# A spectral-mixing stage whose matmuls read each input column four times and write 64 columns instead of 16

## The chip, the cores and the metric

The kernel runs on one core of a Trainium2 chip. The core has a matrix engine (TensorE, in the profile PE for the matmuls and PEld for the loads of their stationary operand), a vector engine (VectorE, DVE), a scalar engine (ScalarE, ACT), GpSimd (POOL), a queue engine (SyncE, SP) and 16 DMA engines. The metric is the device time of one execution in microseconds (us), the median of several executions. The kernel before took 380.24 us (three executions, 378.93 to 380.4).

## The reference

Two stages run one after the other on `x`, 8 batches of 5696 positions and 128 features. The first is a long convolution with `h`, done by FFT. The second is a spectral mixing: the first 64 modes of the real FFT along the sequence are each multiplied by their own complex 128 x 128 matrix, the result goes back through the inverse FFT, is added to its input, and a gated linear layer is added to that.

```
Xf = rfft(x, n=2*S); Hf = rfft(h, n=2*S)
x  = irfft(Xf * Hf)[:, :S]                       # S = 5696
X  = rfft(x);  Xr, Xi = X[:, :64].real, X[:, :64].imag
Yr = einsum('bmd,mde->bme', Xr, w_r) - einsum('bmd,mde->bme', Xi, w_i)
Yi = einsum('bmd,mde->bme', Xr, w_i) + einsum('bmd,mde->bme', Xi, w_r)
u  = x + irfft(Y, n=S)                           # Y is zero above mode 64
out = u + relu(u @ w_ch)
```

## The kernel before

The FFTs are products with constant matrices. The sequence is split into 89 rows of 64 positions, and the two steps of the transform, the pointwise product with the filter and the way back are all matmuls with fp16 operands and fp32 sums in PSUM. PSUM has eight banks of 512 fp32 values in each of 128 partitions; every result is copied out of it by ACT or DVE (the helper `evac`, lines 301 to 314).

The program is written as one list of operations for each engine in the order of the code. A `Recorder` (lines 21 to 121) notes what each operation reads and writes by name (a PSUM bank is `("bank", i)`) and puts in the semaphore waits that follow. So the order of the matmuls on PE is the order of the calls, and a matmul that needs a bank waits until the engine that was to read the bank has done so. All matmuls go through the helper `mm`, so nearly all have line 320 in the profile, and are told apart by their operands' names.

The stages are, in order: the transform of `h` (`ps<-F,Hp`), four groups of two batches, each with the transform of `x` and the convolution (`ps<-F,Xin`, `ps<-As,M`, `ps<-U,Wc`) and the gathering of the 64 modes (`ps<-G,Zs`), and the last part, from about 257 us on. There the modes of all batches lie in the tile XT: for each batch 192 values in a row, the imaginary parts with changed sign, the real and the imaginary ones, 64 each.

The change is made at the start of that last part, in lines 770 to 798. `reflect` fills the second half of two constant tiles (S4a on DVE, S4b on ACT). `mix(m0, m1)` does the mixing: for each mode two matmuls with the mode's 128 x 128 matrices from the tile W as stationary operand (`ps<-XT,W`). The moving operand is read out of XT with the step from batch to batch: 8 batches, 192 fp16 values (384 bytes) apart, for the real and the imaginary part, 16 columns in all. The 16 columns that come out lie next to one another in bank 6 (modes 0 to 31) or bank 7 (32 to 63). In between PE does parts of the way back from the convolution, `u_z` (`ps<-S4a,ZT0a` and `ps<-S4b,ZT0b`, 89 columns each), for three tiles ahead, in banks 0 to 5. Two copies, one on ACT and one on DVE, bring the mixed modes of a bank to the tile Y (`Y<-ps`). Then eight transposes (line 791, `ps<-Id,Y`) turn Y into banks 6 and 7, two more copies scale this into the tile C, and from there `u_tile` and `o_tile` alternate until the end: the way back of the modes is added (`ps<-IBs,C`, 356 columns), the sum is copied to UT, and the gated layer (`ps<-WI,UT`) and the output follow. The first column blocks of `u_z` go to the slots of two banks 0, 2, 4, 6 in turn (`LSLOT`), so the third tile ahead has banks 4 and 5.

GpSimd and SP issue DMAs only here: GpSimd loads the gated layer's weights and the tiles ZT3 and ZT4, SP later loads and the output.

Of the kernel before, what the change touches and what calls it, by code (L numbers as in the profile page):

```python
# [4 lines left out]
P = 128  # L5
# [8 lines left out]
RELU = mybir.ActivationFunctionType.Relu  # L14
# [109 lines left out]
def bass_long_conv_fft__then__afno_spectral_mix_kernel(nc, x, h, moe_w_r, moe_w_i, moe_w_ch, out):  # L124
    B, S, D = x.shape
    M = moe_w_r.shape[0]
# [79 lines left out]
    def at(name, cols, dt, off):  # L206
        return nc.alloc_sbuf_tensor_at(name, [P, cols], dt, offset=off)
# [41 lines left out]
    XTW = 3 * M  # L249
    xt = at("XT", B * XTW, F16, a_g + GW * 2 + 2048 * (NZX - NZ))  # L250
# [24 lines left out]
    NR = len(r_off)  # L275
    r_sb = [at(f"R{i}", 512, F32, r_off[i]) for i in range(NR)]
    w_sb = at("W", 2 * M * D, F16, a_x)
    y_sb = at("Y", 2 * B * M, F16, r_off[0])
# [10 lines left out]
    def pv(bank, off, dims, p0=0, n=P):  # L289
        return bass.AP(ps, p0 * 4096 + bank * 512 + off, [[4096, n]] + [list(d) for d in dims])  # L290

    R = Recorder(nc)
# [3 lines left out]
    def bank(i):  # L296
        return ("bank", i)
# [3 lines left out]
    def evac(dst, src, reads, writes, scale=None, eng=None, after=()):  # L301
        e = eng
        if e is None:
            turn[0] ^= 1
            e = "scalar" if turn[0] else "vector"
        if e == "scalar":
            if scale is None:
                R.add(e, lambda h_: h_.copy(dst, src), reads, writes, after=after)  # L308
            else:
                R.add(e, lambda h_: h_.activation(dst, src, COPY, scale=scale), reads, writes, after=after)  # L310
        elif scale is None:
            R.add(e, lambda h_: h_.tensor_copy(dst, src), reads, writes, after=after)  # L312
        else:
            R.add(e, lambda h_: h_.tensor_scalar_mul(dst, src, scale), reads, writes, after=after)  # L314

    def dma(eng, dst, src, ring, reads=(), writes=(), after=()):
        R.add(eng, lambda h_: h_.dma_start(dst, src), reads, writes, ring=ring, after=after)  # L317

    def mm(o, l, r, st, sp, reads, writes):
        R.add("tensor", lambda h_: h_.matmul(o, l, r, start=st, stop=sp), reads, writes)  # L320
# [3 lines left out]
    def once(key, toks):  # L324
        if key in first:
            return []
        first[key] = 1
        return list(toks)
# [3 lines left out]
    def turns(name, items):  # L332
        i = ring2.get(name, 0)
        ring2[name] = i + 1
        return items[i % len(items)]
# [80 lines left out]
    for j in range(16):  # L416
        t = turns("h", [0, 2, 4])
        for i in range(8):
            d = 8 * j + i
            for r in range(2):  # L420
# [6 lines left out]
             eng="vector" if j % 4 == 1 else "scalar")  # L427
# [69 lines left out]
    G_ALL = [("g", i) for i in range(NG)]  # L497
    WT = [("w", i) for i in range(NWP)]
    ZY = [("zs", i, b) for i in range(NZL, NZX) for b in range(2)]
# [18 lines left out]
    def reflect(eng, t, n, col, key, after):  # L518
        MN = S - SH
        dst, src = bass.AP(t, SH, [[S, n], [1, MN]]), bass.AP(t, SH - NQ - 1, [[S, n], [-1, MN]])  # L520
        sc = sg_sb[0:n, col:col + 1]
        if eng == "scalar":
            R.add(eng, lambda e: e.activation(dst, src, COPY, scale=sc), [key + (0,), ("sg",)], [key + (1,)], after=after)
        else:
            R.add(eng, lambda e: e.tensor_scalar_mul(dst, src, sc), [key + (0,), ("sg",)], [key + (1,)], after=after)
# [201 lines left out]
    def u_z(i, b, half, alone=False, parts=(0, 1)):  # L727
        g_, c_ = divmod(i, NCH)
        t = ahead.get((i, b, half))
        if t is None:  # L730
            t = turns("l", LSLOT)
        z = zt[i % NC]
        for hb in parts:
            if not alone:
                u_c(i, b, half, t, hb, True)
            for pl in range(4):
                for ri in range(2):
                    pz = half * 8 + hb * 4 + pl
                    so = (c_ * ZB + pz) * NQ
                    n = (P, PB + RB)[ri]  # L740
                    mm(pv(t + hb, pl * NQ, [[1, NQ]]), z[ri][0:n, pz * 256 + b * P:pz * 256 + b * P + P], s4_sb[ri][0:n, so:so + NQ],
                       alone and pl == 0 and ri == 0, not alone and pl == 3 and ri == 1, [("zt", i % NC, ri), ("zt0", i % NC), ("s4", ri, 0)] + ([("s4", ri, 1)] if c_ >= NCH // 2 else []), [bank(t + hb)])
        if alone:
            ahead[(i, b, half)] = t
        return t
# [24 lines left out]
    XTT = [(n, g_) for g_ in range(NP) for n in ("xt", "xtn")]  # L770
    reflect("vector", s4_sb[0], P, 0, ("s4", 0), M_ALL[1:4])
    reflect("scalar", s4_sb[1], PB + RB, 1, ("s4", 1), AST)
    def mix(m0, m1):
        for m in range(m0, m1):
            for ri, first_col in ((0, M + m), (1, m)):
                mm(pv(6 + m // 32, m % 32 * 2 * B, [[1, 2 * B]]), w_sb[:, (ri * M + m) * D:(ri * M + m + 1) * D],
                   bass.AP(xt, first_col, [[B * XTW, P], [M, 2], [XTW, B]]), ri == 0, ri == 1, WT + XTT, [bank(6 + m // 32)])

    u_z(0, 0, 0, True)
    for n in range(2):  # L780
        mix(16 * n, 16 * n + 16)
        u_z(0, 0, 1, True, (n,))
    mix(32, M)
    u_z(0, 1, 0, True, (0,))
    for hb in range(2):
        evac(bass.AP(y_sb, hb * 32 * B, [[2 * M * B, P], [B, 32], [M * B, 2], [1, B]]),
             pv(6 + hb, 0, [[2 * B, 32], [B, 2], [1, B]]), [bank(6 + hb)], [("y", hb)], eng="vector" if hb else "scalar",
             after=ZY)
    for b in range(B):
        bk = 6 + b // 4  # L790
        R.add("tensor", lambda e, b=b, bk=bk: e.transpose(  # L791
            ps16[:, bk * 1024 + (b % 4) * P:bk * 1024 + (b % 4) * P + P], bass.AP(y_sb, b, [[2 * M * B, P], [B, P]]), id_sb[:, :]),
              [("y", 0), ("y", 1), ("id",)], [bank(bk)])
    u_z(0, 1, 0, True, (1,))
    for hb in range(2):
        evac(c_sb[:, hb * 512:hb * 512 + 512], ps16[:, (6 + hb) * 1024:(6 + hb) * 1024 + 512], [bank(6 + hb)],
# [11 lines left out]
    def o_tile(g_, b, r4):  # L808
        ub = (g_ % 2) * 2 + b
        bb = 2 * g_ + b  # L810
        t = turns("l", LSLOT)
        i = n_o[0]
        n_o[0] += 1
        full = r4 < NW // 4
        last_ = (g_, b) == (NP - 1, 1)
        wide = r4 < (8 if last_ else NW // 4 // 2 * 2)
        big = wide or (last_ and full)
        h_ = r4 % 2 if wide else 0
        if big:
            if not h_:  # L820
                o_cur[0] = turns("o8", list(range(NO8)))
            ob, key, old = o8_sb[o_cur[0]], ("o8", o_cur[0]), o8_old[o_cur[0]]
        else:
            k_ = turns("os", list(range(NO)))
            ob, key, old = o_sb[k_], ("os", k_), o_old[k_]
        OW = 1024 if big else 512
        n, rows = (4, P) if full else (1, TAIL)
        rd = [("u_", ub, c_) for c_ in range(2 * NCH)] + [("wch",), ("i16",)]
        for j in range(n):
            lh = bass.AP(u_sb[ub], 4 * r4 + j, [[S, P], [NW, P]]) if full else u_sb[ub][:, NW * P:S]  # L830
            mm(pv(t + j // 2, (j % 2) * 256, [[1, 256]], 0, rows), lh, WI, True, True, rd, [bank(t + j // 2)])
        bk = [bank(t), bank(t + 1)] if full else [bank(t)]
        rs = r_sb[i % NR]
        rv = bass.AP(rs, 0, [[512, rows], [P, n], [1, P]])
        ov = bass.AP(ob, h_ * 512, [[OW, rows], [P, n], [1, P]])
        src_r, src_u = pv(t, 0, [[256, n], [1, P]], 0, rows), pv(t, P, [[256, n], [1, P]], 0, rows)
        R.add("scalar", lambda e: e.activation(rv, src_r, RELU), bk, [("r", i % NR)], after=once(("r", i % NR), G_ALL + XTT + [("y", 0), ("y", 1), ("id",)]))  # L837
        R.add("vector", lambda e: e.tensor_tensor(ov, src_u, rv, ADD), bk + [("r", i % NR)],  # L838
              [key + (h_,)], after=once(key, old))
        if wide and not h_:  # L840
            return
        w_ = (2 if wide else 1) * 4 * D
        if full:
            dst = bass.AP(out.tensor, out.offset + bb * S * D + (4 * r4 - 4 * h_) * D, [[NW * D, P], [1, w_]])
            src = ob[:, 0:w_]
        else:
            dst = bass.AP(out.tensor, out.offset + bb * S * D + NW * P * D, [[D, TAIL], [1, D]])
            src = ob[0:TAIL, 0:P]
        dma("sync", dst, src, "o", [key + (v_,) for v_ in range(h_ + 1)])
# [4 lines left out]
    for g_ in range(NP):  # L854
        last = g_ == NP - 1
        order = [(c_, b) for b in range(2) for c_ in range(NCH)] if last else [(c_, b) for c_ in range(NCH) for b in range(2)]
        for n, (c_, b) in enumerate(order):
            i = NCH * g_ + c_
# [10 lines left out]
    while todo:  # L869
        o_tile(*todo.pop(0))  # L870
# [32 lines left out]
```

## Time and profile before

| | |
|---|---|
| median of three executions | 380.24 us |
| profiled execution, its own time | 383.51 us |
| profiled execution, span | 381.7 us |
| busy: PE, PEld | 363.6 us (95%), 280.4 us (73%) |
| busy: DVE, ACT, POOL | 303.7 us (80%), 311.9 us (82%), 83.9 us (22%) |
| mixing matmuls (`ps<-XT,W`) | 128, first start 257.7 us, last start 262.1 us |
| copies to Y | ACT 585 ns, DVE 693 ns |
| chain that ended last | PE 82%, ACT 9%, DVE 6% |

The profile is of one execution. "Busy" counts the time in which an engine has an instruction in flight. Matmuls overlap, so the time from the start of one to the start of the next is shorter than the duration of one, and a PE that is always busy need not be at its peak. PEclk is the TensorE clock that was granted, as a share of the full one. A group's row shows the line, the engine, the operation, the tile written and the tiles read, the shapes, the number of instructions, the busy time in us and the mean duration of one in ns, and behind the second bar the idle time of the engine before them and what ended it.

### The profile page before, as it was taken

The numbers are of one execution on the slowest core, as the hardware profiler recorded it, in microseconds if no ns is written. First come the engines' busy times: TensorE is split into PE (matmuls) and PEld (weight loads), VectorE is DVE, ScalarE is ACT, GpSimd is POOL, SyncE is SP. The second block draws the span as 40 slices with busy tenths as digits, with TensorE's granted clock in tenths as the row PEclk, the third lists the DMA queues.
The fourth block names the chain that finished last, engine by engine and source line by source line (L and its number), as shares of the span: only waits on it lengthen the run. The fifth ranks groups of instructions, "written<-read, shape, count | busy, mean of one in ns | idle before, by whom it ended". The sixth has DMA issues, their size and how long they took to land.

```text
span 381.7 us, 11950 instructions
## 1 busy us (share of the span) xinstructions
PE 363.6 (95%) x5107; PEld 280.4 (73%) x5107; DVE 303.7 (80%) x331; ACT 311.9 (82%) x492; POOL 83.9 (22%) x137
## 2 busy tenths in 40 slices
PE   7998989999989999999999899999999999999992
PEld 4898856667856667766668666668898988888871
DVE  7566998998988998889998888766347766777784
ACT  8357989998989998999998899994466777777783
POOL 8400012320823311822203211339000000000000
PEclk9997999999999999999999999996899999999997
DMA  7998589998999996999996599999999999999867
GB/s 137 201 280 349 140 228 227 276 269 238 107 134 228 234 269 167 143 129 250 235 283 119 137 298 251 300 328 406 407 388 402 402 415 414 404 408 378 342 256 313
DMA packets 84560, 103.92 MB, mean 272 GB/s; under 512 B 22126, under 2 KB 68974, under 8 KB 81538
## 3 DMA queue, kind: packets, MB, share of 16 engines
q1 hardware_dynamic: 59643, 67.73, 51.3%
q0 software_dynamic: 24864, 35.43, 44.3%
q8 instruction: 40, 0.66, 0.7%
q14 instruction: 13, 0.11, 0.1%
HBM read 70.61 MB, written 51.12 MB: 319 GB/s over the span
## 4 chain that ended last, share of the span: by engine, by line
PE 82%; ACT 9%; DVE 6%; issue 1%; DMA 0%; DVEq 0%
PE ps L320 82%; ACT As L310 7%; DVE As L314 2%; DVE U L597 1%; DVE Hs L312 1%; ACT R L837 0%; DMA F<-cF 0%; DVE UT L312 0%; ACT UT L308 0%; ACT XT L310 0%; DVE O L838 0%; PE ps L791 0%; ACT Hs L308 0%; DVE Os L838 0%; ACT Ah L310 0%
## 5 line engine op out<-in xcount | busy, mean ns | idle before, releaser
L320 PE MATMUL ps<-U,Wc 128*128 128x512 f16 (+1 forms) x368 | 95.8, 384 | 0.0
L605 DVE TENSOR_TENSOR U<-Xs,Hs 128x2048 f16<-128x2048 f16 (+1 forms) x68 | 80.7, 1189 | 11.5 <-ACT Xs L308 10.0
L308 ACT CAST Xs<-ps 128x1024 f16<-128x1024 f32 (+1 forms) x72 | 69.5, 971 | 7.8 <-PE ps L320 4.8
L838 DVE TENSOR_TENSOR O<-ps,R 128x512 f32<-128x512 f32 x81 | 52.5, 686 | 19.8 <-ACT R L837 12.5
L308 ACT CAST Zs<-ps 128x512 f16<-128x512 f32 (+1 forms) x126 | 66.0, 604 | 0.0
L837 ACT ACTIVATE R<-ps 128x512 f32<-128x512 f32 x96 | 50.9, 573 | 14.6 <-PE ps L320 14.1
L314 DVE TENSOR_SCALAR As<-ps 128x720 f16<-128x720 f32 (+1 forms) x60 | 50.1, 879 | 9.1 <-PE ps L320 8.0
L310 ACT ACTIVATE As<-ps 128x720 f16<-128x720 f32 (+1 forms) x72 | 51.6, 772 | 6.6 <-PE ps L320 5.7
L320 PE MATMUL ps<-F,Xin 128*128 128x180 f16 x512 | 54.5, 255 | 2.6 <-ACT Ah L310 1.0
L320 PEld LDWEIGHTS ps<-F,Xin 128*128 128x128 f16 x512 | 46.8, 156 | 9.3 <-DVE As L314 2.6
L320 PE MATMUL ps<-WI,UT 128*128 128x256 f16 x360 | 52.5, 281 | 0.5 <-DVE O L838 0.4
L320 PE MATMUL ps<-As,M 64*128 64x128 f16 x1440 | 48.9, 217 | 4.3 <-DVE U L597 3.5
L320 PEld LDWEIGHTS ps<-U,Wc 128*128 128x128 f16 x368 | 28.5, 98 | 28.5 <-ACT Zs L308 6.1
L320 PEld LDWEIGHTS ps<-As,M 64*128 64x128 f16 x1440 | 40.5, 94 | 10.9 <-DVE U L597 4.2
L317 POOL DMA_DIRECT2D Xt<-in_x_dram x48 | 24.8, 520 | 102.9 <-PE ps L320 102.2
L605 DVE TENSOR_TENSOR U<-ps,Hs 128x2048 f16<-128x2048 f32 x20 | 45.7, 2283 | 0.0
L308 ACT CAST UT<-ps 128x712 f16<-128x712 f32 x40 | 30.0, 752 | 18.7 <-PE ps L320 18.7
L320 PEld LDWEIGHTS ps<-WI,UT 128*128 128x128 f16 x360 | 39.5, 152 | 4.4 <-issue 2.2
L320 PE MATMUL ps<-IBs,C 128*128 128x356 f16 x128 | 40.8, 328 | 0.4
L320 PEld LDWEIGHTS ps<-G,Zs 128*128 128x128 f16 x492 | 27.3, 97 | 13.3
L308 ACT CAST Zt<-ps 128x512 f16<-128x512 f32 (+1 forms) x58 | 31.0, 606 | 0.1
L320 PE MATMUL ps<-G,Zs 128*128 128x2 f16 (+2 forms) x492 | 30.5, 192 | 0.0
(88 smaller groups left out, 500.3 us busy)
## 6 DMA issues: line engine op xcount, KB each, us to landing
out_dram<-O SPq DMA_DIRECT2D x39, 512.0 KB, 10.4
zscr<-Zs SPq DMA_DIRECT2D x60, 256.0 KB, 6.3
Xt<-in_x_dram POOLq DMA_DIRECT2D x24, 320.0 KB, 6.9
zscr<-Zt SPq DMA_DIRECT2D x28, 256.0 KB, 6.6
W<-wscr POOLq DMA_DIRECT2D x8, 512.0 KB, 5.3
M<-cM POOLq DMA_DIRECT2D x5, 720.0 KB, 20.3
ZT0a<-zscr SPq DMA_DIRECT2D x3, 1024.0 KB, 13.4
Xr<-in_x_dram POOLq DMA_DIRECT2D x8, 320.0 KB, 13.8
```

What stands on the lines that cost most here:

```text
L308: R.add(e, lambda h_: h_.copy(dst, src), reads, writes, after=after)
L310: R.add(e, lambda h_: h_.activation(dst, src, COPY, scale=scale), reads, writes, after=after)
L312: R.add(e, lambda h_: h_.tensor_copy(dst, src), reads, writes, after=after)
L314: R.add(e, lambda h_: h_.tensor_scalar_mul(dst, src, scale), reads, writes, after=after)
L317: R.add(eng, lambda h_: h_.dma_start(dst, src), reads, writes, ring=ring, after=after)
L320: R.add("tensor", lambda h_: h_.matmul(o, l, r, start=st, stop=sp), reads, writes)
L597: R.add("vector", lambda e, b=b, s_=s_: e.tensor_tensor(bass.AP(u_s[i], b * 512, [[2048, P], [1024, 2], [1, n * D]]), s_, hv, MULT), [tok, ...
L605: R.add("vector", lambda e: e.tensor_tensor(uv, src, hv, MULT), bk + [("h", t, 0), ("h", t, 1, 0), ("h", t, 1, J)], [("u", i)])
L837: R.add("scalar", lambda e: e.activation(rv, src_r, RELU), bk, [("r", i % NR)], after=once(("r", i % NR), G_ALL + XTT + [("y", 0), ("y", 1 ...
L838: R.add("vector", lambda e: e.tensor_tensor(ov, src_u, rv, ADD), bk + [("r", i % NR)], [key + (h_,)], after=once(key, old))
```

## The change

The mixing's moving operand gets a further dimension of four with a step of zero, so each matmul reads its 16 columns four times and writes 64. The copies lie 64 columns apart in the bank, at the place of the modes four, eight and twelve later, which are written after it in the same bank; the last ones reach beyond the sixteenth mode. 16 modes go to a bank instead of 32, so the mixing uses banks 4 to 7. Four copies to Y of 256 columns each, alternating between ACT and DVE and each behind its 16 modes, take the place of two copies of 512 columns behind all modes. The transposes wait for all four, and the first use of a tile that lies over Y is ordered behind all four.

```
+    MQ = M // 4
+
     def mix(m0, m1):
         for m in range(m0, m1):
             for ri, first_col in ((0, M + m), (1, m)):
-                mm(pv(6 + m // 32, m % 32 * 2 * B, [[1, 2 * B]]), w_sb[:, (ri * M + m) * D:(ri * M + m + 1) * D],
-                   bass.AP(xt, first_col, [[B * XTW, P], [M, 2], [XTW, B]]), ri == 0, ri == 1, WT + XTT, [bank(6 + m // 32)])
+                mm(pv(4 + m // MQ, m % MQ * 2 * B, [[8 * B, 4], [1, 2 * B]]), w_sb[:, (ri * M + m) * D:(ri * M + m + 1) * D],
+                   bass.AP(xt, first_col, [[B * XTW, P], [0, 4], [M, 2], [XTW, B]]), ri == 0, ri == 1, WT + XTT, [bank(4 + m // MQ)])
+
+    def y_out(q):
+        evac(bass.AP(y_sb, q * MQ * B, [[2 * M * B, P], [B, MQ], [M * B, 2], [1, B]]),
+             pv(4 + q, 0, [[2 * B, MQ], [B, 2], [1, B]]), [bank(4 + q)], [("y", q)], eng="vector" if q % 2 else "scalar",
+             after=ZY)
 
     u_z(0, 0, 0, True)
     for n in range(2):
-        mix(16 * n, 16 * n + 16)
+        mix(MQ * n, MQ * n + MQ)
+        y_out(n)
         u_z(0, 0, 1, True, (n,))
-    mix(32, M)
+    for n in range(2, 4):
+        mix(MQ * n, MQ * n + MQ)
+        y_out(n)
     u_z(0, 1, 0, True, (0,))
-    for hb in range(2):
-        evac(bass.AP(y_sb, hb * 32 * B, [[2 * M * B, P], [B, 32], [M * B, 2], [1, B]]),
-             pv(6 + hb, 0, [[2 * B, 32], [B, 2], [1, B]]), [bank(6 + hb)], [("y", hb)], eng="vector" if hb else "scalar",
-             after=ZY)
     for b in range(B):
         bk = 6 + b // 4
         R.add("tensor", lambda e, b=b, bk=bk: e.transpose(
             ps16[:, bk * 1024 + (b % 4) * P:bk * 1024 + (b % 4) * P + P], bass.AP(y_sb, b, [[2 * M * B, P], [B, P]]), id_sb[:, :]),
-              [("y", 0), ("y", 1), ("id",)], [bank(bk)])
+              [("y", q) for q in range(4)] + [("id",)], [bank(bk)])
```

More of the change, by code (lines that the diff above doesn't have):

```diff
@@ L836, in o_tile @@
         src_r, src_u = pv(t, 0, [[256, n], [1, P]], 0, rows), pv(t, P, [[256, n], [1, P]], 0, rows)
-        R.add("scalar", lambda e: e.activation(rv, src_r, RELU), bk, [("r", i % NR)], after=once(("r", i % NR), G_ALL + XTT + [("y", 0), ("y", 1), ("id",)]))
+        R.add("scalar", lambda e: e.activation(rv, src_r, RELU), bk, [("r", i % NR)], after=once(("r", i % NR), G_ALL + XTT + [("y", q) for q in range(4)] + [("id",)]))
         R.add("vector", lambda e: e.tensor_tensor(ov, src_u, rv, ADD), bk + [("r", i % NR)],
```

## The prediction

> **What bounds the kernel now.** I read the page first, then the chain of waits in order of time, then the busy time by stretches around the mixing, and last the groups with their shapes kept apart. The page:
>
> ```profile
> span 381.7 us, 11950 instructions
> PEclk9997999999999999999999999996899999999997
> ```
>
> The chain that ended last, in order of time (start, length, what):
>
> ```profile
> 257.70 5.23 PE ps L320 x152
> 262.93 0.23 issue
> 263.16 1.05 PE ps L791 x8
> 264.21 29.32 PE ps L320 x437
> ```
>
> PE itself is the bound from the mixing on: four further pieces of 9 to 13 us follow with gaps below 0.1 us, up to 343 us, and most of what is left is PE too. No wait of PE in this stretch is for a DMA. So what PE gains or loses between 257.7 and 268.4 us reaches the end nearly whole. In the clock's row the slices from 257.6 to 276.7 us stand out (6 and 8). The stretches, for PE alone the first three numbers (length, busy, count), then PEld, DVE, ACT, POOL, the granted clock, DMA share and GB/s:
>
> ```profile
> 22.68:26.10 3.42, 3.42 (x63) 3.42 (x61) 2.19 (x3) 1.94 (x3) 0.00 (x0) 0.95 1.05 259
> 26.10:29.51 3.41, 2.46 (x43) 2.37 (x42) 1.50 (x2) 1.91 (x3) 0.00 (x0) 0.95 0.99 405
> 29.51:32.92 3.41, 3.41 (x24) 3.41 (x25) 1.73 (x2) 1.78 (x3) 0.00 (x0) 0.50 1.03 428
> ...
> 258.20:261.62 3.42, 3.42 (x114) 3.42 (x111) 2.92 (x1) 2.21 (x2) 3.42 (x4) 0.95 1.06 427
> 261.62:265.03 3.41, 3.18 (x51) 2.86 (x48) 1.48 (x3) 0.60 (x1) 3.41 (x5) 0.50 1.00 400
> 265.03:268.44 3.41, 3.41 (x25) 2.27 (x24) 1.33 (x3) 1.41 (x2) 2.94 (x3) 0.50 1.07 389
> 268.44:271.86 3.42, 3.42 (x64) 3.06 (x63) 1.78 (x2) 1.15 (x2) 0.00 (x0) 0.95 1.06 423
> ```
>
> The clock falls to 0.50 at 261.6 us and comes back at 268.4, a stay of 6.8 us; the only other stay before the end is 29.5 to 32.9, half as long, and the two beginnings are 68 times 3.41 us apart. PE is *busy* throughout 258.20 to 261.62, and the clock falls all the same: 98 of its 114 matmuls have 16 columns, and 98 x 16 + 16 x 89 = 2992 columns at 0.42 ns (slope below) fill 1.25 us, 37% of the stretch. Before the other fall it was 43 x 90 x 0.42 = 1.6 us, 48%, where 70% (63 matmuls) had kept the clock in the stretch before. So what counts is not whether PE is busy but how much of the time columns pass.
>
> **What a column costs.** Durations of groups, shapes kept apart (count, busy us, mean ns):
>
> ```profile
> L320 PE MATMUL ps<-IBs,C 128*128 128x356 f16 x21 | 6.6, 315 | 0.0
> L320 PE MATMUL ps<-G,Zs 128*128 128x128 f16 x246 | 28.7, 216 | 0.0
> L320 PE MATMUL ps<-G,Zs 128*128 128x2 f16 x152 | 15.5, 166 | 0.0
> L320 PE MATMUL ps<-XT,W 128*128 128x16 f16 x128 | 4.3, 192 | 0.1
> ...
> L320 PEld LDWEIGHTS ps<-WI,UT 128*64 128x64 f16 x8 | 0.8, 106 | 1.2 <-issue 1.0 <-ACT UT L308 0.2
> L320 PEld LDWEIGHTS ps<-F,Hp 128*64 128x64 f16 x256 | 15.2, 214 | 0.3 <-issue 0.3
> ```
>
> The first (from 270 to 280 us, at full clock) to third read adjacent columns: (315 - 166) / 354 = 0.42 ns a column on a base of 165. Sixteen such columns would take 172 ns; the mixing's take 192. They lie 384 bytes apart in XT. So each costs 0.42 + 20/16 = 1.69 ns, four times an adjacent one. Loads of the stationary operand show the same: 64 adjacent columns 106 ns, 64 columns 260 bytes apart (Hp) 214, 1.69 ns more for each; for 128 columns it is 98 (Wc) against 156 (Xin), 0.45 ns more each.
>
> ```profile
> 260.24 1.98 PEld L320 LDWEIGHTS ps<-XT,W 128*128 128x128 f16 x64
> 260.28 2.05 PE L320 MATMUL ps<-XT,W 128*128 128x16 f16 x64
> 262.37 0.69 DVE L312 CAST Y<-ps 128x512 f16<-128x512 f32 x1 [1.25 <-PE ps L320]
> 263.13 0.82 PEld L791 LDWEIGHTS ps<-Id,Y 128*128 128x128 f16 x8 [0.41 <-issue]
> ```
>
> From the timeline: the 64 starts are (2.05 - 0.19) / 63 = 29.5 ns apart, which is 27 ns for the columns and 2.5 between matmuls. After the fall the last of them, from 261.87 us on, start every 26 to 27 ns, not every 55: the slow reading does not go by PE's clock. Nor does the load of Xin: 156 ns in the whole trace, 167 at 0.50, where adjacent loads go from 98 to 151.
>
> **The change part by part.** *64 columns in place of 16.* The repeat reads the same 384-byte steps again, so I count 64 x 1.69 = 108 ns and 2 between, 110 ns a matmul while the clock is full and 107 when it is half (27 ns for 16 columns there). Bounds from the rows: with 0.45 ns extra a column, 64 x 0.87 + 2.5 = 58 ns; with 1.69 extra, 64 x 2.11 + 2.5 = 138. I take the middle one, because it is measured on this very operand. Sum on PE: first 32 matmuls 3.52 us, the 8 matmuls of `u_z` 0.34 as now, the next 32 3.42, `u_z` at half clock 0.59 (rows start every 74 ns there, 42 at full clock), the last 64 6.83: 14.70 us, where 257.70 to 262.17 is 4.47. That is +10.23 (bounds +3.7 and +13.9). Writing in four separate runs costs nothing: `ps<-G,Zs` matmuls that scatter 4 columns take 169 ns.
>
> [...]
>
> *Does the clock stay up?* Not by this count. 64 columns in 110 ns use 64 x 0.42 = 27 ns of array time, 24%, hardly more than the 23% of 16 in 29.5. So the clock falls as now, at the end of the first stretch that is mostly mixing, costs little inside it, and the matmuls behind it run at half clock as now: nothing gained, nothing lost, within the 1.7 us that one stretch of 3.41 us more or less at half clock is worth, by where the end of the mixing falls between the marks. Here it falls on the same place: 10.23 is three times 3.41.
>
> *The copies.* The last mixing copy is on DVE before and after; its 512 columns take 693 ns, the 128-column one to XT on DVE 292, so 256 take 426. The transposes start 0.69 + 0.07 us after the copy's start, later than the end of the eight `u_z` matmuls that cover it (262.72); now that gap of 0.41 shrinks by 0.26: **-0.26**. The three other copies (0.38 us on ACT, where 256 columns to XT take 379 ns; 0.43 on DVE) run beside the mixing, behind the reflections that end at 259.83 and 261.12; if one were late, banks 4 and 5 would hold up `u_z` in them, but they are copied 7 us before.
>
> *Banks.* Banks 4 and 5 were last copied out at 256.5 us, before the mixing starts: nothing. DMA and both issuing queues: POOL's and SP's instructions stay as they are, none waits for the mixing before the first load into ZT0's place, which shifts with the work; ZT1 to ZT4 land earlier against it. *The end* follows: +10.23 - 0.26 = **+9.97 us**. The profiled span goes from 381.7 to 391.7, its own time (383.51, 0.9% above the median shown) to 393.5, and the median from 380.24 to **390.2**.
>
> **The rivals.** *The change does what its form suggests: faster.* The repeated reads cost no more than adjacent columns, 64 x 0.42 + 2.5 = 29.4 ns a matmul, so the mixing stays at 3.8 us, array time becomes 91% and the clock stays at 0.95. Behind C's first use (264.6 to 268.4 us), 9 IBs matmuls save 0.145 each (297 ns apart at half clock, 152 at full) and 16 of `u_z` 0.032: 1.82 us. Before it the copy to C becomes the wait: 0.20 to the last copy to Y, 0.43 for it, 0.07, four transposes 0.22, 0.20 until ACT has them, 0.60 for the copy and 0.06 make 1.78 us from the mixing's end, where it is 2.44 now: 0.66. Together 2.5, less up to 0.2 for a slower step: 377.9, -0.6%. It decides from where a matmul is below 29.5 + 2500 / 128 = 49 ns, 0.73 ns a column. For it speaks that the addresses repeat; against it the 192 ns. [...] Chance 0.08.
>
> *A stall at the start of a matmul, not per column.* The 20 ns are paid once: 20 + 27 + 2.5 = 49 ns, mixing +2.5 us, clock kept (55%, between the 48 that lost it and the 70 that kept it), -2.5: 380.2. Against it: loads grow with the number of columns. 0.05.
>
> *Slow reading, but the clock stays up* because time spent reading counts as activity: +10.2 - 2.5, and 0.25 less for `u_z` between the mixing's parts: 387.7. Against it: 258.20 to 261.62 was busy to 100% and the clock fell. 0.07.
>
> *Slow reading doubled by the half clock:* 215 ns for the matmuls after the fall, some 400 us. Against it the fifteen per quarter microsecond. 0.03.
>
> **How the numbers follow.** My forecast has 0.77. The range 386.5 to 394 takes in sums from 1.2 ns a column up to the bound of 138 ns a matmul, the marks' 1.7 us around the forecast and the third rival; the lower bound of 58 ns would end near 383 and is left to the tail; it leaves out the first, second and fourth (0.16) and little else. A difference of 0.5% (1.9 us) is about what can be told from no change: faster 0.09, within 0.04, slower 0.87.
>
> **What would show it.** Right: `ps<-XT,W` has 128x64 with a mean near 273 ns (165 + 108), starts 107 to 110 ns apart, the mixing ends near 272.4 us, the clock is 0.50 from about 261.6 to 278.7, and later stretches are copies of those before, 10 us later. Wrong in the reading: a mean near 192 ns and starts 30 ns apart. Wrong in the clock: 0.95 right through. Wrong in the copies: PE waiting for ACT or DVE ahead of a `u_z` in banks 4 or 5.

## The result and the profile after

The changed kernel takes **389.34 us** (median of five executions, 387.78 to 390.04), the kernel before 379.98 on the same chip (five executions, 378.93 to 380.4). The ratio is 1.0245, with a 95% interval of 1.0216 to 1.0274: 9.36 us slower, where 9.97 was forecast, and 389.3 where 390.2 was. The profiled execution took 390.04 us, its span is 388.3.

The page of the changed kernel, the span and the clock's row:

```profile
span 388.3 us, 11952 instructions
PEclk9999999999999999999999999995899999999999
```

There is one slow place now, slices 28 and 29, where the row of before had one at slice 4 as well (and a 7 in the last slice). The chain of waits around the mixing (start, length, what):

```profile
254.70 1.02 PE ps L320 x18
255.72 0.15 issue
255.88 15.84 PE ps L320 x152
271.72 1.01 PE ps L797 x8
272.73 27.11 PE ps L320 x432
```

It is the same chain with one piece longer: 152 matmuls took 5.23 us and take 15.84. The groups of the mixing and of its copies (count, busy us, mean ns of one, then the idle time before):

```profile
L320 PE MATMUL ps<-XT,W 128*128 128x64 f16 x128 | 14.7, 288 | 0.1
...
L312 DVE CAST Y<-ps 128x256 f16<-128x256 f32 x2 | 0.8, 424 | 11.4 <-PE ps L320 11.4
L308 ACT CAST Y<-ps 128x256 f16<-128x256 f32 x2 | 0.7, 372 | 9.2 <-PE ps L320 9.2
```

The timeline of the mixing, its last copy and the first load for the transposes (start, length, then what, and how many in a row):

```profile
255.88 3.69 PE L320 MATMUL ps<-XT,W 128*128 128x64 f16 x32
259.74 3.69 PE L320 MATMUL ps<-XT,W 128*128 128x64 f16 x32
263.82 7.29 PE L320 MATMUL ps<-XT,W 128*128 128x64 f16 x64
...
270.94 0.26 PE L320 MATMUL ps<-S4a,ZT0a 128*128 128x89 f16 x1
...
271.15 0.42 DVE L312 CAST Y<-ps 128x256 f16<-128x256 f32 x1 [7.26 <-PE ps L320]
271.65 0.83 PEld L797 LDWEIGHTS ps<-Id,Y 128*128 128x128 f16 x8
```

A row's length is from the first start to the last end, and one matmul lasts 0.29 us: the starts lie (3.69 - 0.29) / 31 = 110 ns apart in the first row, and as much in the second. The stretches between the marks of the clock (start:end, length; PE, PEld, DVE, ACT and POOL busy with counts; granted clock, DMA share, GB/s):

```profile
256.80:260.22 3.42, 3.42 (x39) 3.42 (x37) 2.48 (x1) 1.57 (x2) 3.42 (x5) 1.00 1.05 418
260.22:263.63 3.41, 3.41 (x36) 3.41 (x34) 0.17 (x1) 0.00 (x0) 3.41 (x5) 0.50 1.01 407
263.63:267.05 3.42, 3.42 (x35) 3.42 (x33) 0.26 (x1) 0.00 (x0) 1.95 (x2) 0.50 1.09 391
267.05:270.46 3.41, 3.41 (x33) 3.41 (x32) 0.00 (x0) 0.37 (x1) 0.00 (x0) 0.50 1.00 407
270.46:273.87 3.41, 3.41 (x33) 2.98 (x32) 1.53 (x3) 0.60 (x1) 0.00 (x0) 0.50 0.81 329
273.87:277.29 3.42, 3.42 (x58) 2.84 (x56) 1.89 (x3) 2.13 (x3) 0.00 (x0) 1.00 0.51 129
```

PE is busy without a gap, and the clock is halved for four of these stretches, from 260.22 to 273.87. So the first 32 mixing matmuls ran at full clock, most of the next 32 and all of the last 64, (7.29 - 0.29) / 63 = 111 ns apart, at half.

**Where the time went, in the two profiles.** From the mixing's first start to the start of the `u_z` matmuls behind its last it is 15.07 us (255.88 to 270.94) against 4.47 (257.70 to 262.17): **+10.6**. The two rows of before are:

```profile
257.70 1.11 PE L320 MATMUL ps<-XT,W 128*128 128x16 f16 x32
...
262.17 0.24 PE L320 MATMUL ps<-S4a,ZT0a 128*128 128x89 f16 x1
```

From there to the end of the span it is 117.3 against 119.5: -2.2. And the mixing starts 1.82 us earlier. Together 388.3 - 381.7 = +6.6. The last two terms belong in part to the execution of before that was profiled: at 29.5 us its clock fell for one mark, 28 matmuls `ps<-F,Xin` took 4.02 us there and 2.68 in the profile after, and its own time, 383.5, lies 3.5 above the median of before. So the medians (+9.36) and not the two profiles give the size.

### The profile page after: what moved, and what is told of

Read it like the earlier page. It is cut to its first block, busy times and chain, and to the rows that moved or that the text cites. A ratio compares the mean times of both kernels' runs of the same rounds, so it can differ in the third digit from the quotient of the medians.

```text
span 388.3 us, 11952 instructions
## 1 busy us (share of the span) xinstructions
PE 370.0 (95%) x5107; PEld 287.4 (74%) x5107; DVE 302.9 (78%) x332; ACT 311.4 (80%) x493; POOL 83.7 (22%) x137
## 4 chain that ended last, share of the span: by engine, by line
PE 81%; ACT 10%; DVE 6%; issue 1%; DMA 0%; DVEq 0%
PE ps L320 81%; ACT As L310 7%; DVE As L314 3%; ACT R L843 1%; DVE U L597 1%; ACT UT L308 1%; DVE Hs L312 1%; DVE O L844 1%; DMA F<-cF 0%; DVE UT L312 0%; ACT XT L310 0%; ACT Hs L308 0%; PE ps L797 0%; ACT Ah L310 0%; DVE Os L844 0%
## 5 line engine op out<-in xcount | busy, mean ns | idle before, releaser
L320 PE MATMUL ps<-U,Wc 128*128 128x512 f16 (+1 forms) x368 | 94.4, 376 | 0.0
L320 PE MATMUL ps<-F,Xin 128*128 128x180 f16 x512 | 52.8, 249 | 2.8 <-ACT Ah L310 0.9
L320 PEld LDWEIGHTS ps<-F,Xin 128*128 128x128 f16 x512 | 45.1, 155 | 9.7 <-DVE As L314 2.7
L320 PE MATMUL ps<-IBs,C 128*128 128x356 f16 x128 | 39.6, 318 | 0.7
```

## The experiments

The theory is that of the prediction: each column read at a step of 384 bytes costs 1.7 ns, a repeat costs it again, and the clock falls because few columns pass. The rivals are a stall once per matmul, a cost that goes by the distance, and parts of the change that have nothing to do with the reading (four banks and four copies).

### c64: the same 64 columns, laid next to one another

XT is laid out by value, the eight batches as neighbours, so that each repeat reads two runs of eight adjacent columns.

```
-        evac(bass.AP(xt, 2 * g_ * XTW + M, [[B * XTW, P], [XTW, 2], [1, P]]), pv(MB, 0, [[P, 2], [1, P]]),
+        evac(bass.AP(xt, M * B + 2 * g_, [[B * XTW, P], [1, 2], [B, P]]), pv(MB, 0, [[P, 2], [1, P]]),
...
-                   bass.AP(xt, first_col, [[B * XTW, P], [0, 4], [M, 2], [XTW, B]]), ...
+                   bass.AP(xt, first_col * B, [[B * XTW, P], [0, 4], [M * B, 2], [1, B]]), ...
```

> The changed kernel with XT laid out the other way round: the 8 batches of a mode lie next to each other, so the moving operand's 16 columns are two runs of 8 adjacent values, still read four times, 64 columns written. Theory (a column read at a wide step costs 1.7 to 1.9 ns, an adjacent one 0.42; the clock falls when columns pass for too small a share of the time): ps<-XT,W has a mean near 192 ns (165 + 64 x 0.42) and starts about 30 ns apart, the mixing takes 4.5 us with the u_z in it, the clock stays full through and behind it, and the time is 377.5 us, some 2.5 below the kernel before. Rival 1 (the cost is the repeat with step zero or the four separate runs written to PSUM): starts stay 110 ns apart, 389 us. Rival 2 (the clock falls for another reason than the columns, such as the many loads of the stationary operand): starts 30 ns apart, but the clock still goes to 0.50, and the time is that of before, 380.

Measured: 384.01 us, 1.0101 of before (1.0068 to 1.0134). The matmuls take 193 ns and start 29 ns apart, in place of 288 and 110: with the same number of columns, repeats, banks and copies, only the layout is another. The clock does not fall at the mixing. Its row of the page:

```profile
PEclk9999999999999999999999999999999999999997
```

So both halves of the theory hold here, and yet the kernel is slower than before. The groups that write XT, and the start of the mixing in the timeline, say why:

```profile
L310 ACT ACTIVATE XT<-ps 128x256 f16<-128x256 f32 x4 | 5.2, 1308 | 0.3 <-PE ps L320 0.3
L310 ACT ACTIVATE XT<-ps 128x128 f16<-128x128 f32 x3 | 3.2, 1079 | 0.0
L314 DVE TENSOR_SCALAR XT<-ps 128x128 f16<-128x128 f32 x1 | 0.7, 723 | 3.5 <-ACT XT L310 3.5
```

```profile
260.18 1.09 PE L320 MATMUL ps<-XT,W 128*128 128x64 f16 x32 [1.48 <-ACT XT L310]
```

The writers now put each value 16 bytes behind the one before, and take 1308, 1079 and 723 ns where the old layout takes 376, 285 and 293. The last of them lies right ahead of the mixing: PE waits 1.48 us for ACT. At the three earlier groups of batches PE waits another 4.4 us in all for these copies (0.2 in the changed kernel), and the mixing starts at 260.2 in place of 255.9. The price was moved from the reader to the writers.

### c16: the new layout alone, 16 columns read once

> The kernel before with only the layout of XT changed: 16 columns, read once, as two runs of 8 adjacent values. Theory: mean 172 ns instead of 192, starts 26 ns apart instead of 29.5, the mixing 0.4 us shorter; the clock falls as before (16 x 0.42 = 6.7 ns of 26 are columns), so 379.5 us, not to be told from before. Rival 1 (no cost of the step): mean stays 192. Rival 2 (a matmul busy with reading counts as idle, and adjacent reading alone keeps the clock up): clock stays full and 377.5 us.

The kernel before with c64's XT. 385.25 us, 1.0135 (1.0098 to 1.0172).

```profile
PEclk9998999999999999999999999995899999999997
```

```profile
261.20 1.00 PE L320 MATMUL ps<-XT,W 128*128 128x16 f16 x32 [1.51 <-ACT XT L310]
```

A matmul takes 175 ns (before: 192), which is close to the 172 that the prediction worked out for 16 adjacent columns, so the 20 ns of before are the step's. The clock is halved for 10.2 us from 261.2, which is the mixing's first matmul: it falls behind a stretch in which PE waited for ACT, and stays down while columns pass for 34% of the time. With the same writers c64 has four times the columns and is 1.2 us faster by the medians, though their intervals overlap. The profiles say the same: the second part of `u_z` begins 3.9 us behind the last mixing start there and 6.0 here, and from the last mixing start to the end of the span it is 117.7 us there and 118.9 here. The two also differ by the copies to Y (0.27 us, see b4). So the full clock behind the mixing is worth at most about 1.2 us at the end of these two profiles, half of the first rival's 2.5.

### steps_a and steps_b: one column's price by its step

64 columns as in the changed kernel, 16 values read four times over, but in a row with a step of 2, 4, 8 and 16 bytes (steps_a) and of 12, 32, 64 and 192 bytes (steps_b), one step for each bank's modes.

```
+    STEPS = (1, 2, 4, 8)          # steps_b: (6, 16, 32, 96)
...
-                   bass.AP(xt, first_col, [[B * XTW, P], [0, 4], [M, 2], [XTW, B]]), ...
+                   bass.AP(xt, m, [[B * XTW, P], [0, 4], [STEPS[m // MQ], 2 * B]]), ...
```

> The changed kernel, but the moving operand reads 16 values of XT at one step, four times over, from other places than the mixing needs, so the mixing's result is not the reference's: modes 0 to 15 at a step of 1 value (2 bytes), 16 to 31 at 2 (4 bytes), 32 to 47 at 4 (8 bytes), 48 to 63 at 8 (16 bytes). Theory: starts 30 ns apart at step 1, 110 ns at step 8 if every column then pays in full; the steps between show where the cost begins. If the cost goes by the bytes of a 16-byte piece, step 2 and 4 cost little or in proportion; if any step beyond 1 costs in full, they are at 110 ns too. Rival (the cost comes from 384 bytes being a special distance, such as the same bank of the memory): step 8 stays near 30 ns.

> The kernel of the four steps with wider ones, 16 values at a step read four times; again the mixing's result is not the reference's: modes 0 to 15 at a step of 6 values (12 bytes), 16 to 31 at 16 (32 bytes), 32 to 47 at 32 (64 bytes), 48 to 63 at 96 (192 bytes). Theory (the cost is one 16-byte piece for nearly every column, whatever lies between): about 85 to 95 ns at 12 bytes, where three of four columns open a new piece, 110 at the other three. Rival (it grows with the distance, or 384 bytes are special): 32, 64 and 192 bytes differ by more than 5 ns.

The timeline of steps_a:

```profile
255.65 1.15 PE L320 MATMUL ps<-XT,W 128*128 128x64 f16 x32
256.98 1.34 PE L320 MATMUL ps<-XT,W 128*128 128x64 f16 x32
258.50 5.90 PE L320 MATMUL ps<-XT,W 128*128 128x64 f16 x64
```

and of steps_b:

```profile
255.89 3.05 PE L320 MATMUL ps<-XT,W 128*128 128x64 f16 x32
259.33 3.96 PE L320 MATMUL ps<-XT,W 128*128 128x64 f16 x32
263.69 7.24 PE L320 MATMUL ps<-XT,W 128*128 128x64 f16 x64
```

Taken apart by bank (the last row of each fence holds two steps), with the changed kernel as the last column of the table:

| step, bytes | 2 | 4 | 8 | 12 | 16 | 32 | 64 | 192 | 384 |
|---|---|---|---|---|---|---|---|---|---|
| start to start, ns | 30.9 | 36.7 | 62.7 | 89.5 | 116 | 118 | 110.5 | 110.3 | 110 |
| mean duration, ns | 193 | 200 | 241 | 269 | 295 | 298 | 287 | 287 | 288 |

The price climbs up to a step of 16 bytes and not beyond; at 64 bytes and more it is 6 to 8 ns lower again. 64 columns at one step each open a 16-byte piece of SBUF at (110 - 2.5) / 64 = 1.68 to (118 - 2.5) / 64 = 1.80 ns; at 12 bytes three pieces hold four values, (89.5 - 2.5) / 48 = 1.81 ns a piece; at 8 bytes two values share one, 60.2 / 32 = 1.88. At 2 bytes the columns' own 0.42 ns set the time (64 x 0.42 + 2.5 = 29.4 of the 30.9). A cost that goes by the distance is out: 32 bytes and 64 differ by 7.5 ns, more than the 5 that were named as this rival's sign, but the greater distance is the cheaper, and 64, 192 and 384 agree. Why 16 and 32 bytes cost the 6 to 8 ns more stays open. A stall once per matmul is out as well: the number of matmuls and columns is the same in all nine. The times, one execution each, follow the sum: 383.17 us for steps_a, 389.68 for steps_b.

### b4 and b4_5: four banks and four copies without the repeat

```
-                mm(pv(4 + m // MQ, m % MQ * 2 * B, [[8 * B, 4], [1, 2 * B]]), ...
-                   bass.AP(xt, first_col, [[B * XTW, P], [0, 4], [M, 2], [XTW, B]]), ...
+                mm(pv(4 + m // MQ, m % MQ * 2 * B, [[1, 2 * B]]), ...
+                   bass.AP(xt, first_col, [[B * XTW, P], [M, 2], [XTW, B]]), ...
```

> The changed kernel with the repeat taken out: four banks and four copies to Y of 256 columns, but 16 columns read once at the old steps. Theory: mean 192 ns and starts 29.5 ns apart as before, the clock falls as before, the last copy to Y takes 0.43 us instead of 0.69 and the transposes start 0.26 us earlier behind the mixing's end; 379.7 us, not to be told from before. Rival (using banks 4 and 5 holds PE up, or the copies between delay something): PE waits ahead of a u_z for ACT or DVE, and the time is above before.

> The kernel with four banks and four copies but 16 columns read once, this time timed. Theory: transposes start 0.26 us earlier behind the mixing, clock falls as before: 0.1% below the kernel before, not to be told from it. Rival: the single run of 377.83 was no luck, and the copies bring 1 us or more.

A single execution (b4) took 377.83 us; twelve of the same kernel (b4_5) have a median of 380.18 against 380.46: 0.9993 (0.9972 to 1.0015). The first number lies below the lowest of the twelve (378.55), at the low end of the scatter. The step itself does what it should. The timeline of b4_5:

```profile
260.09 0.42 DVE L312 CAST Y<-ps 128x256 f16<-128x256 f32 x1 [0.96 <-PE ps L320]
260.59 0.51 PEld L797 LDWEIGHTS ps<-Id,Y 128*128 128x128 f16 x5
```

The transposes start 0.75 us behind the last mixing matmul's start, 1.02 before: 0.27 won. PE waits for no bank, and the matmuls are those of before (192 ns, 29.7 apart). So the four banks and copies are worth a quarter of a microsecond at their place and nothing that the time can tell; the whole loss is the repeated reading.

### a48 and a64: fewer 16-byte pieces with the layout of before

In place of reading the 16 values four times, three (a48) or four (a64) adjacent modes are read for each of the 16, so that two to four columns come from one piece. The output is the same.

```
-                mm(pv(4 + m // MQ, m % MQ * 2 * B, [[8 * B, 4], [1, 2 * B]]), ...
-                   bass.AP(xt, first_col, [[B * XTW, P], [0, 4], [M, 2], [XTW, B]]), ...
+                mm(pv(4 + m // MQ, m % MQ * 2 * B, [[1, 2 * B], [8 * B, NR_]]), ...
+                   bass.AP(xt, first_col, [[B * XTW, P], [M, 2], [XTW, B], [1 if m < M - NR_ else -1, NR_]]), ...
```

> XT in its old layout, which its writers fill in 0.38 and 0.29 us, and four banks as in the changed kernel, but the three columns of a value are three adjacent modes (read with step 1, or -1 at the last modes) instead of the same one three times: 48 columns, 16 jumps. The two further columns are another mode's input under this mode's weights; they land where the repeat's copies would and are written over, and the result is the reference's. Theory (the cost is per 16-byte piece that is opened, about 1.8 to 2.2 ns with up to four values of it, by the starts of 37 ns with four values a piece in the kernel of four steps): starts about 36 ns apart, mixing 0.8 us longer than before, 48 x 0.42 = 20 of 36 ns are columns, with u_z 62% of a stretch of 3.41 us, the clock stays full, 2.5 us less behind the mixing: 378.7 us, some 1.7 below the kernel before. Rival 1 (the writing of values 64 columns apart in PSUM is slow): starts 60 ns or more apart and 382 us. Rival 2 (62% is too little): the clock falls and the time is 381.

> The same with four adjacent modes: 64 columns, 16 jumps. Theory: starts 37 to 44 ns apart, mixing 1.0 to 1.8 us longer than before, columns for over 60% of the time, the clock stays full: 379 us, 1 below the kernel before. Rival 1 (slow writing): 70 ns or more. Against the changed kernel with its 110 ns it differs only in where the 64 columns are read and in the order of writing, so the 10 us are the reading's if they go.

a48: 381.39 against 380.46, 1.0037 (1.0012 to 1.0062). a64: 383.01, 1.0068 (1.0044 to 1.0091). The timelines' rows for the last 64 matmuls, a48 first:

```profile
258.82 3.04 PE L320 MATMUL ps<-XT,W 128*128 128x48 f16 x64
```

```profile
259.33 3.75 PE L320 MATMUL ps<-XT,W 128*128 128x64 f16 x64
```

The starts lie 44.7 and 55.8 ns apart, more than the 36 and 37 to 44 expected; the pieces alone don't explain it. The starts of single matmuls say more. In a48 six modes of eight have their three values inside one 16-byte piece and start every 42.5 ns; the two whose values lie across two pieces take 47 to 59. In a64 the modes that stay inside a piece start every 56 ns. So most of the excess is there without a second piece, and 42.5 and 56 ns are 2.5 and 0.83 ns for each column, twice the 0.42 of adjacent columns. The step of 4 bytes in steps_a has four values to a piece as well and takes 36.7 ns. That leaves the writing, where every next column goes 64 columns further in the bank (p64, below, writes pairs side by side and takes 31.3); no run changes the writing alone, so this cause is argued and not shown.

In the stretches of the mixing columns pass for 48% (a48) and 51% (a64) of the time or more, counting the columns of the matmuls that start in a stretch at 0.42 ns, and **the clock stays up**, where 36% (before) and 31% (after) let it fall. The full clock does not pay for the longer mixing (+2.0 and +3.4 us), and both kernels miss the 378.7 and 379 us that were expected of them. In a48 there is a second, accidental cost, seen in the timelines of GpSimd, of DVE and of PE behind it:

```profile
263.10 1.82 POOL L513 MEMSET ZT4b<- 32x2048 uint32 x1
263.49 2.17 DVE L525 TENSOR_SCALAR IBs<-IBs,SG 128x2759 f16<-128x2759 f16 x1
...
266.51 0.32 PE L320 MATMUL ps<-IBs,C 128*128 128x356 f16 x1 [0.89 <-DVE UT L312]
```

The reflection of IBs takes 0.93 us where no memset runs beside it and 2.17 here, where it starts while GpSimd's memset runs; the copy behind it on DVE is late, and PE waits 0.9 us.

### p64: free reading at last

The two batches of a group become neighbours in XT, so that a matmul reads runs of eight adjacent values (two batches of four modes) and the writers put pairs side by side, reading PSUM at a step in place of writing SBUF at one.

```
-        evac(bass.AP(xt, 2 * g_ * XTW + M, [[B * XTW, P], [XTW, 2], [1, P]]), pv(MB, 0, [[P, 2], [1, P]]),
+        evac(bass.AP(xt, 2 * g_ * XTW + 2 * M, [[B * XTW, P], [2, P], [1, 2]]), pv(MB, 0, [[1, P], [P, 2]]),
...
-                   bass.AP(xt, first_col, [[B * XTW, P], [0, 4], [M, 2], [XTW, B]]), ...
+                   bass.AP(xt, 2 * (first_col - (0 if up else 3)), [[B * XTW, P], [2 * M, 2], [2 * XTW, NP], [1, 8]]), ...
```

> Four banks and 64 columns as in the changed kernel, but XT holds the two batches of a group as neighbours (the copies that fill it write adjacent values and read PSUM at a step of 512 bytes instead), and the further columns are the next three modes instead of a repeat: a matmul reads 8 runs of 8 adjacent values (16 bytes). The result is the reference's. Theory (about 2.2 ns for a 16-byte piece with four values, 3.4 with eight; runs lie across one or two pieces): starts 29 to 40 ns apart, mixing 0 to 1.3 us longer than before, clock full through and behind it. Behind the mixing the kernel then gains what the stays at half clock cost, 0.8 us for one of 3.4 us and 2.4 for one of 6.8 by the starts of the second chunk in the runs so far, and 0.26 by the copies: 379.3 us, 1 below the kernel before, if the copies to XT keep their 0.38 and 0.29 us. Rival 1 (reading PSUM at a step is as slow as writing at one was, 1.3 us a copy): 383 us. Rival 2 (gains ahead of 270 us do not reach the end, because the loads of ZT come too late for them): chunk starts earlier up to the twelfth, and the time is that of before.

The mixing's group, and the clock's row of the page:

```profile
L320 PE MATMUL ps<-XT,W 128*128 128x64 f16 x128 | 4.5, 194 | 0.0
```

```profile
PEclk9999999999999999999999999999999999999999
```

64 columns in 194 ns, starts 31.3 apart, the writers at 377, 285 and 292 ns as before, the mixing 4.7 us long, and the clock full from the first matmul to the last: everything that the first rival wanted. The time is 380.1 against 379.94, **0.9996 (0.9966 to 1.0027)**: no change. The way back runs through twenty ZT tiles, 0 to 19. From the last mixing start to the first matmul of tile 12 it takes 69.7 us here, 72.0 in the profile of before, 71.1 in b4_5 and 70.3 in b4: p64 is 0.6 to 2.3 us ahead there, most against before, whose stay at half clock was the longest of these. Two tiles later 1.7 us of that are gone against before: from tile 13 to tile 14 it takes 5.7 us, and 4.0 in the profile of before. DVE's waits from 320 to 360 us (us in total, times, longest), and its timeline there:

```profile
DVE O L845 <- DMA out_dram<-O: 2.3, 1, 2.3
```

```profile
338.23 1.29 DVE L845 TENSOR_TENSOR O<-ps,R 128x512 f32<-128x512 f32 x2 [2.34 <-DMA out_dram<-O]
```

DVE waits for an output tile whose DMA has not landed; in the profile of before there is no such wait (b4_5 has two, 1.8 us in all, and c64 one of 0.9). The DMA engines are busy to 100% from 320 to 342 us, before as here. From the last mixing start to the end p64 needs 117.65 us and the profile of before 119.6, but the changed kernel needs 117.4 with 2.9 us of half clock left behind the mixing, b4 116.6 and b4_5 119.0 with stays of 3.4. Single profiles differ here by as much as there is to win. The medians say that the start ahead of time is not handed through to the end; that waits like this one are what keeps it back is not shown by these profiles.

### before_less and p64_less: is it the DMAs that take the gain back?

Both kernels without the output DMAs of the first three batches (8.7 of 103.9 MB), so that the last part has free transfers.

```
-        dma("sync", dst, src, "o", ...)
+        if bb >= 3:
+            dma("sync", dst, src, "o", ...)
```

> The kernel before without the output's DMAs of the first three of eight batches (8.7 of 103.9 MB left out; everything is computed). Theory (DMA is full from 257 to 355 us, but PE sets the end): less than 1 us below the kernel before, 379.5 us. Rival (the DMAs set the end): 2 us or more below.

> The kernel that reads runs of 8 adjacent values and keeps its clock, without the same DMAs. Theory (what it gains behind the mixing is taken back around 336 us, where a copy to an output tile waits 2.3 us for that tile's last DMA): without that wait it is 1 to 2 us below the kernel before that leaves out the same DMAs. Rival (the gain is lost elsewhere, or there is none): as long as that kernel, within 0.5 us.

before_less: 378.48 against 380.26, 0.9954 (0.9935 to 0.9972). p64_less: 377.58, 0.9933 (0.9911 to 0.9956). The kernel before alone gets 1.8 us shorter without these transfers (the interval is 1.1 to 2.5), where the theory had less than 1 and its rival 2 or more: the theory that PE alone sets the end misses. A stretch of p64_less:

```profile
302.00:322.00 20.00, 19.82 (x282) 17.48 (x281) 14.09 (x22) 14.63 (x26) 0.00 (x0) 1.00 0.62 228
```

The DMA share is 0.62 there, and no wait for an output is left. Without the outputs p64 is 0.8 us ahead of before, by the means of six executions each (377.74 and 378.57, about 0.7 either way); with them it is 0.2 behind. That goes in the direction of the theory put down for p64_less, but lies between what it and its rival named, and the interval nearly reaches zero. That full DMAs take back part of what p64 wins is likely by this and seen at one wait in one profile; how much it is stays open.

No version is faster than before: b4_5 and p64 are equal to it.

## Why the prediction was right

*PE is the bound from the mixing on, and what it loses reaches the end.* Right for the loss: +10.6 us in the mixing, +9.36 in the time. For a gain "reaches the end nearly whole" does not hold: p64 was 0.6 to 2.3 us ahead 70 us behind the mixing, depending on the profile that it is held against, and its median is that of before; its own profile shows 1.7 us lost at one wait for an output's DMA. Nor is PE the only bound: without the outputs of three batches the kernel before is 1.8 us shorter.

*110 ns a matmul.* Measured 110 at full clock and 111 at half (forecast 107). The sum of 14.70 us for the mixing came out at 15.07, and most of the difference is the part at half clock. (The 1.69 ns a column is 27 / 16; the sum written beside it, 0.42 + 20/16, gives 1.67, which is 1 ns a matmul less.) The step behind it, that a repeat with step zero pays the full price again, is shown by c64: the same repeat over adjacent columns costs 29 ns. What it goes by are pieces of 16 bytes, and the two step runs show that: 30.9 ns a matmul where eight columns share a piece, 62.7 where two do, 116 at a step of 16 bytes and no rise beyond it (118 to 110). That is about 1.75 ns for every piece opened. The *mean duration* was off: 273 forecast, 288 measured. I had added the 108 ns of columns to a base of 165 ns, so that duration and spacing grow alike; from a step of 2 bytes to one of 384 the spacing grows by 79 ns and the duration by 95. It entered no sum.

*The slow reading does not go by PE's clock.* Right, by the rows of 3.69 us: one at full clock, one mostly at half.

*The clock falls as now and costs nothing more.* It fell as forecast at the first mark after the mixing filled a stretch, and it did cost little inside the mixing. That stretch, with 28 starts of the mixing and 8 of `u_z`, had 31% of column time; the 24% of the forecast are the mixing's alone, and hold for 267.05 to 270.46. (The prediction's shares count every matmul that is in flight in a stretch. By those that start in it, its 37% are 36 and its 48% are 42, and nearly all matmuls of the latter stretch are `ps<-F,Hp`, whose stationary operand has 64 columns and not 128, so it can't be set beside the mixing's.) It came back one mark sooner than forecast, at 273.87. The last mark inside the mixing lay 0.5 us ahead of its end, as before, but the stretch behind that mark was enough to bring the clock back, and was not in the profile of before: with the shorter way to C, 2.6 of the wide matmuls `ps<-IBs,C` fit in ahead of the next mark, where it was 1.5. With them columns passed for 46% of that stretch, and for 43% in before. That is a count of starts; that it decided is argued. So the half clock lasted 2.9 us behind the mixing and not 6.3. The 1.7 us that I had kept for one stretch more or less held it.

*Copies and banks.* Forecast -0.26; the transposes follow the last mixing start by 0.85 us and 1.02 before, -0.17, and -0.27 in b4_5. The copies took 372 and 424 ns (379 and 426 forecast). No wait for banks 4 or 5.

*The sum.* +9.97 forecast, +9.36 measured (1.0216 to 1.0274 of 379.98 is 8.2 to 10.4). Its largest term was 0.4 too small, and "nothing gained" behind the mixing was about 1 us too large; the two errors partly cancel, and that much of the closeness is luck. In the profiles that part is -2.2, but the profile of before had a stay of 6.8 us, twice those of b4 and b4_5; what a usual execution of before loses there was not seen, so the split of the last microsecond is argued and not shown. For the same reason the forecast of the profiled execution, 393.5, was 3.5 too high: it was made against an execution with a stay at 29.5 us, which the profiled execution of the changed kernel does not have.

*The rivals.* The first fell at 110 ns, far over its 49; and p64 adds that with its premise fulfilled the time is 380.1 and not 377.9: its 2.5 us were priced at their place, from a profile with a long stay, and not followed to the end. The stall once per matmul is out by the table of steps (the loads that were held against it do not grow with their columns alone: 64 adjacent ones take 106 ns, 128 take 98). Slow reading with the clock up is out by the stretches: PE was busy to 100% with slow reading, and the clock fell. The doubling by half clock is out by 111 against 110.

## What to carry to other kernels

Price a matmul's moving operand by the 16-byte pieces it opens (about 1.75 ns each here) when that is more than its columns (0.42 ns each), and count a repeat with step zero again in full (110 ns here for four times the columns that took 29.5); a group whose duration lies above the slope of adjacent columns shows it (192 ns here in place of 172). A layout that makes the reader fast must be priced at its writers too: ACT and DVE took 3.5 and 2.5 times as long when they wrote at a 16-byte step (1308 ns for 376, 723 for 293), and no longer when they read PSUM at a step of 512 bytes (377 and 292). And follow a gain to the end, not to the edge of its stage: of the one or two microseconds that the profiles show won in a stretch where PE was the bound, the median showed none, and in one profile most went seventy microseconds later at a wait for a DMA.

## What was not expected of the hardware

- The clock falls although PE is busy (after: 3.42 of 3.42 us from 256.80 to 260.22, then 0.50). Around the mixing, the share of a stretch of 3.41 us in which columns pass (those of the matmuls that start in it, at 0.42 ns each) tells what comes next in all these profiles: behind 24 to 42% (steps_a, c16, after, b4_5, b4, before, steps_b, before_less) the clock was halved, behind 45% and more (the stretch ahead of it in b4_5 and in after, and those of a48, a64, c64 and p64) it was full. Elsewhere the share does not decide alone. b4 and a48 lost the clock behind stretches full of `ps<-F,Hp`, with 64% and 62%, behind which the other profiles kept it (these matmuls take 302 and 310 ns on average there, 295 in the others); and c16 and c64 kept it, twice each, behind 38 to 44% of `ps<-F,Xin` and others, where PE was idle for over 40% of the stretch. What else counts is not shown.
- Writing fp16 into SBUF at a 16-byte step: ACT 256 columns 1308 ns in place of 376, DVE 128 columns 723 in place of 293. Reading PSUM at a 512-byte step with pairs written side by side: 377 ns, no cost.
- DVE's reflection hardly gets on while GpSimd's memset runs: it ends 0.74 or 0.75 us behind the memset. The changed kernel's timelines of DVE and of GpSimd:

```profile
255.69 3.60 DVE L525 TENSOR_SCALAR S4a<-S4a,SG 128x2759 f16<-128x2759 f16 x1
```

```profile
254.98 1.82 POOL L513 MEMSET ZT1b<- 32x2048 uint32 x1
256.72 1.82 POOL L513 MEMSET ZT2b<- 32x2048 uint32 x1
```

It ends at 259.29, which is 0.75 us behind the end of the second memset (258.54). In the profile of before it ends 0.74 behind it (3.60 us long), in c64 0.74 (2.52 long); the reflection of IBs does so in a48 (2.17 long), in p64 (1.15) and in b4_5 (1.01), and lasts 2.05 in c16. With no memset beside it, it takes 0.93 (after, c64). The end goes by the memset's end and not by its own start: the 0.74 us that are left behind the memset are the same for an overlap of 0.27 us (b4_5) and of 2.86 (before). So, by these ends, it does not run slower, it waits; what makes it wait is not shown.
